# Loading q and k of heads 0 to 3 in two token ranges, and storing the last rows in three pieces, in a sliding-window attention and gated MLP kernel

## Chip, cores and metric

The kernel runs on one core of a Trainium2 chip. The metric is the time of one execution on the device in microseconds (us), here the median of three. Lower is better.

## The reference

Causal attention over a window of 64 tokens (8 batches, 8 heads, 576 tokens, head size 64), and behind it a gated MLP on the 4608 tokens of width 512 with 1536 hidden units. Inputs and output are fp32.

```python
scores = scale * np.matmul(q, k.transpose(0, 1, 3, 2))
rel = pos[:, None] - pos[None, :]
mask = (rel >= 0) & (rel < 64)
scores = np.where(mask, scores, -1e9)
attn = softmax(scores)                       # max taken off, sum + 1e-9
x = np.matmul(attn, v).transpose(0, 2, 1, 3).reshape(B * S, H * D)
gate = np.maximum(x @ w_gate, 0.0)
return gate * (x @ w_val) @ w_out            # [4608, 512]
```

## The kernel before

**Units and tiles.** Attention is computed in units of 192 tokens (`U`), three to a batch, later in quads of 256. The MLP works on tiles of tokens: four of 384 (two units each), then six of 512. A unit goes through `u_st` (scores, transposed, as 64-token blocks against 128 keys), `u_exp` (ScalarE), a mask or, for units 0 and 1, a bias that `u_bias` puts into PSUM ahead of the scores, `u_pv` (probabilities times values, with a column of ones that yields the sum), `u_recip` and `u_norm` (VectorE) and `u_turn`, a VectorE transpose that writes the tile `xt` that the MLP reads. `hidden` multiplies `xt` with the gate and value weights into PSUM tiles of one bank each (pool `f_ps`, four banks in rotation), ScalarE applies the relu (L453), VectorE multiplies the two (L456) into `g_sb`, and `out_mm` multiplies that with the output weights. The 12 chunks of 128 hidden units are counted by f.

**Loads.** q, k, v and the weights come in through GpSimd's DMA queue (L148, L150, L167, L191), which casts fp32 to fp16 on the way. The exceptions are q and k of batch 0, heads 0 to 3 (`G` = 4 heads on 128 partitions, 32 partitions per head): `first_load` (L169) fetches each as one fp32 transfer of 128 rows of 4608 bytes on SyncE's queue (L172), and `first_round` (L174) casts it to fp16, half of the columns on VectorE and half on ScalarE. `qk_trans` (L180) then transposes blocks of 32 x 32 pairs on VectorE into `kT` and `qT`, which the scores read. A partition holds 18 consecutive tokens of a head. Heads 4 to 7 (`hh` = 1) are loaded by GpSimd (`qk_load`) right after and take only the transpose.

**Order of the work.** Every engine works through its instructions in the order in which the program writes them. The head of the kernel (L537 to L590) is written out by hand: loads, constants, bias, casts and transposes of k and q, scores and exps of units 0 and 1, `v_spread` (copies values to the other half of the partitions, VectorE for unit 0, GpSimd for unit 1), `u_pv` and normalisation of both units. Units 0 and 1 are tokens 0 to 383 of batch 0; unit 2, its last 192 tokens, is planned later. After that a planner, `Weaver`, takes over: `W.at(t, fn)` puts a piece of work at time t of a clock that counts TensorE's matmuls and the estimated landing of weights (`w_need`), and `hidden` and `out_mm` write out whatever has come due before each group of their own matmuls. So the plan's times fix only the order in each engine's stream. Relus and gates are put into the plan at the clock of their matmuls. From `W.advance(15.3)` (L660) on, the first tile's hidden chunks f = 0 to 3 come in two spans of 192 tokens (gate weights for both spans, then value weights for both), then chunks 4 to 11 with 384 tokens at a time. Unit 2's scores are planned at 26.0 (L591).

**The last rows.** `output_last` (L505) computes the last 128 rows in two column halves of 256 (L514), so that the copy and store of the first half run beside the matmuls of the second. The second half is copied in two parts, ScalarE and VectorE, and stored on two queues (L520, L521). The copies use `o_sb`, a pool of three buffers that the earlier output copies (L488) use too.

Of the kernel before, what the change touches and what calls it, by code (L numbers as in the profile page):

```python
# [10 lines left out]
FP32 = mybir.dt.float32  # L11
FP16 = mybir.dt.float16
# [32 lines left out]
def kernel(  # L45
# [10 lines left out]
    nc = tc.nc  # L56
    B, H, S, D = q.shape
    DM = H * D
# [7 lines left out]
    G = 4  # L66
    scale = 1.0 / float(D) ** 0.5
    TT = 2 * U
# [4 lines left out]
    starts = [TT * t for t in range(NS)] + [NS * TT + WT * t for t in range(NL)]  # L73
# [15 lines left out]
    wo = persist.tile([128, NF, DM], FP16)  # L89
# [76 lines left out]
        src = (q if name == "q" else k)[b, G * hh:G * hh + G]  # L166
        nc.gpsimd.dma_start(tile_, src.rearrange("h (i j) d -> (h i) (j d)", i=32))  # L167

    def first_load(name):  # L169

        t32 = nat["32", name] = x_sb.tile([128, S // 32 * D], FP32, name=f"{name}32", bufs=1)
        nc.sync.dma_start(t32, (q if name == "q" else k)[0, 0:G].rearrange("h (i j) d -> (h i) (j d)", i=32))  # L172

    def first_round(name, copies):  # L174
        n = S // 32 * D // len(copies)
        to = nat[0, name, 0] = a_in.tile([128, S // 32 * D], FP16, name=f"{name}0", bufs=2)
        for i, copy in enumerate(copies):
            copy(to[:, n * i:n * i + n], nat["32", name][:, n * i:n * i + n])  # L178

    def qk_trans(b, name, hh, j0=0, j1=S // 32):  # L180

        src = nat[b, name, hh].bitcast(FP32).rearrange("p (j e) -> p j e", e=32)
        dst = qTs[b % 2][:, hh] if name == "q" else kTs[b % 2][:, hh, 64:64 + S]
        dst = dst.bitcast(FP32).rearrange("p c o -> p (c o)")
        nc.vector.transpose(dst.rearrange("p (i j) -> p j i", i=32)[:, j0:j1], src[:, j0:j1])  # L185
# [8 lines left out]
    def v_spread(u, copy=None, h0=0, h1=H):  # L194

        b, uu = divmod(u, UB)
        t = v16s[b % 2]
        copy = copy or nc.vector.tensor_copy
        for g0, g1 in (((0, 3),), ((4, 5),), ((6, 7),))[uu]:
            copy(t[64:128, g0:g1:2, h0:h1, 0:64], t[0:64, g0 + 1:g1 + 1:2, h0:h1, 0:64])  # L200
        for g0, g1 in (((2, 3),), ((4, 5),), ((6, 9),))[uu]:
            copy(t[0:64, g0:g1:2, h0:h1, 0:64], t[64:128, g0 - 1:g1 - 1:2, h0:h1, 0:64])  # L202
# [73 lines left out]
    def u_pv(u, hhs=(0, 1), banks=None):  # L276

        d = units[u]
        if "pv" not in d:
            if banks:  # L280
                d["pv"] = [one_bank("pv") for _ in range(2)]
            else:
                both = two_banks("pv")
                d["pv"] = [both[:, hh] for hh in range(2)]
                d["both"] = both
        for hh in hhs:
            to = d["pv"][hh]
            for w in range(UB):
                b, vw = divmod(UB * u + w, NG)
                for s in range(2):  # L290
                    for j in range(G):
                        c = VW * (2 * w + s)
                        nc.tensor.matmul(  # L293
                            to[32 * j:32 * j + 32, c:c + D + 1], p_of(u, G * hh + j, w)[:, 32 * s:32 * s + 32],
                            v16s[b % 2][:, vw, G * hh + j, 0:D + 1],
                            start=True, stop=True, skip_group_check=True)
        return 0.27 * len(hhs)
# [195 lines left out]
    def op_tile():  # L493
        return f_ps.tile([128, DM], FP32, name="op", tag="h")
# [10 lines left out]
    def output_last(t):  # L505

        last = widths[t] // 128 - 1
        output(t, range(last))
        W.drain()
        for col in range(2):  # L510
            op = op_tile()
            for f in range(NF):
                g_sb, _ = gs[t]
                nc.tensor.matmul(op[:, 0:256], g_sb[:, f, bass.ds(last * 128, 128)], wo[:, f, 256 * col:256 * col + 256],  # L514
                                 start=(f == 0), stop=(f == NF - 1))
            parts = ((0, 256, nc.scalar.copy, nc.sync),) if col == 0 else (
                (0, 128, nc.scalar.copy, nc.scalar), (128, 256, nc.vector.tensor_copy, nc.sync))
            for c0, c1, copy, queue in parts:
                o_sb = f_sb.tile([128, DM], FP32, name="o_sb")
                copy(o_sb[:, c0:c1], op[:, c0:c1])  # L520
                queue.dma_start(out[bass.ds(starts[t] + last * 128, 128), 256 * col + c0:256 * col + c1], o_sb[:, c0:c1])  # L521

    def output_by_rows(t):
        ops = [op_tile() for _ in range(TT // 128)]
# [8 lines left out]
    with tc.manual_schedule():  # L533
# [170 lines left out]
```

The softmax here doesn't subtract the row's maximum and nothing guards it: scores larger than these inputs give would overflow.

## Time and profile before

The median is 324.95 us (324.91 to 325.01). The profiled execution spans 323.3 us.

| Engine | busy us | share of the span |
|---|---|---|
| TensorE, matmuls | 313.7 | 97% |
| VectorE | 192.1 | 59% |
| ScalarE | 127.0 | 39% |
| GpSimd | 93.7 | 29% |

| Group (line, engine) | number | mean ns | busy us |
|---|---|---|---|
| hidden matmuls (L468, TensorE) | 1088 | 338 and 335 | 223.8 |
| output matmuls (L482, TensorE) | 420 | 379 | 93.9 |
| gate (L456, VectorE) | 120 | 631 | 75.4 |
| transposes of q and k, 128x576 (L185, VectorE) | 32 | 1245 and 1237 | 39.2 |
| output stores (SyncE's queue) | 35 | 2.8 us to landing | |

In the table a row of the profile's groups is one line of the program on one engine; mean ns is the duration of one instruction. Matmuls overlap, so their durations are longer than the distance from one to the next. In lines of the profile "out<-in" names the tile written and the tile read; "idle before, <-releaser" is how long the engine had nothing to do and what ended that. In the timeline a line begins with start and duration in us. A DMA issue has its duration on the issuing engine, and separately the time from issue to landing. For DMA queues, q1 is the queue of SyncE and q0 that of GpSimd; the three figures are packets, megabytes written and the share of the stretch that 16 engines spent on them.

### The profile page before, as it was taken

The page shows a single profiled execution, that of the slowest core. Times are in us where ns is not written, and L with a number is a line of the kernel's source. Part 1 is how long each engine was busy: PE and PEld are TensorE (multiplying, and loading weights), DVE is VectorE, ACT ScalarE, POOL GpSimd, SP SyncE. Part 2 cuts the span into 40 slices and gives each one's busy share as a digit, 9 for nine tenths or more (in the row PEclk, how much of TensorE's full clock was granted, in tenths as well). Part 3 has the DMA queues.
Part 4 walks back from the last instruction along what each step waited for, and adds up shares of the span by engine and source line. Part 5 has one row for each costly group of instructions (what it writes and reads, how often), then busy time and mean ns, then how long its engine had stood idle before and what let it go on. Part 6 is the DMA issues. An engine that isn't in the chain of part 4 may idle for free.

```text
span 323.3 us, 8901 instructions
## 1 busy us (share of the span) xinstructions
PE 313.7 (97%) x3851; PEld 168.4 (52%) x3851; DVE 192.1 (59%) x370; ACT 127.0 (39%) x249; POOL 93.7 (29%) x138
## 2 busy tenths in 40 slices
PE   5699999999999999999999999999999999999995
PEld 2586958656556644454445444454445444544443
DVE  5947962687938749564755656674767146723410
ACT  3444324534424523532454234613372237223321
POOL 8766335285900390029000910071000000000000
PEclk9599999999999999999999999999999999999999
DMA  7999998989590269019900892091001200020002
GB/s 215 186 196 210 194 107 174 155 150 163 83 211 4 15 108 181 3 12 124 214 5 2 111 203 24 2 122 70 0 2 38 97 0 2 21 111 3 0 34 98
DMA packets 52488, 29.48 MB, mean 91 GB/s; under 512 B 38880, under 2 KB 43872, under 8 KB 52448
## 3 DMA queue, kind: packets, MB, share of 16 engines
q0 software_dynamic: 46688, 18.29, 48.4%
q1 hardware_dynamic: 5616, 10.55, 8.9%
q8 instruction: 30, 0.49, 0.6%
q10 hardware_dynamic: 144, 0.07, 0.1%
q14 instruction: 10, 0.08, 0.1%
HBM read 37.75 MB, written 9.44 MB: 146 GB/s over the span
## 4 chain that ended last, share of the span: by engine, by line
PE 94%; DMA 2%; POOL 2%; issue 0%; ACT 0%; DVE 0%; DVEq 0%; POOLq 0%
PE h L468 59%; PE op L482 28%; PE st L233 3%; PE pv L371 2%; DMA v<-in_v_dram 2%; PE pv L293 1%; POOL v L191 1%; DMA out_dram<-o_sb 1%; POOL k L167 0%; POOL v L200 0%; POOL v L202 0%; ACT o_sb L489 0%; POOL q L167 0%; PE st L207 0%; POOL ident L107 0%
## 5 line engine op out<-in xcount | busy, mean ns | idle before, releaser
L456 DVE TENSOR_TENSOR g_sb<-r_sb,h 128x512 f16<-128x512 f32 (+1 forms) x120 | 75.4, 631 | 86.3 <-PE h L468 84.5
L468 PE MATMUL h<-xt,wg 128*128 128x512 f16 (+2 forms) x544 | 112.5, 338 | 0.1
L468 PE MATMUL h<-xt,wv 128*128 128x512 f16 (+2 forms) x544 | 111.3, 335 | 0.0
L453 ACT ACTIVATE r_sb<-h 128x512 f32<-128x512 f32 (+1 forms) x120 | 66.7, 558 | 89.5 <-PE h L468 80.4
L482 PE MATMUL op<-wo,g_sb 128*128 128x512 f16 x420 | 93.9, 379 | 0.0
L468 PEld LDWEIGHTS <-wg 128*128 128x128 f16 x544 | 51.5, 99 | 42.8 <-issue 0.5
L468 PEld LDWEIGHTS <-wv 128*128 128x128 f16 x544 | 50.5, 98 | 40.8
L482 PEld LDWEIGHTS <-g_sb 128*128 128x128 f16 x420 | 40.3, 98 | 47.1
L191 POOL DMA_DIRECT2D v<-in_v_dram x41 | 34.5, 861 | 95.0 <-PE pv L371 90.1
L489 ACT COPY o_sb<-op 128x512 f32<-128x512 f32 x35 | 20.5, 586 | 84.7 <-PE op L482 84.5
L356 DVE TENSOR_TENSOR pw<-pw,mask 128x512 f16<-128x512 f16 x48 | 19.3, 422 | 14.6 <-ACT pw L352 14.3
L352 ACT ACTIVATE pw<-st 128x512 f16<-128x512 f32 x48 | 25.7, 605 | 5.0 <-PE st L233 4.5
L200 POOL COPY v<-v 64x512 f16<-64x512 f16 (+1 forms) x21 | 15.5, 736 | 24.3 <-DMA v<-in_v_dram 23.4
L185 DVE STREAM_TRANSPOSE kT<-k 128x576 f32<-128x576 f32 x16 | 19.9, 1245 | 0.2 <-ACT k L178 0.2
L185 DVE STREAM_TRANSPOSE qT<-q 128x576 f32<-128x576 f32 x16 | 19.3, 1237 | 0.1
L267 ACT ACTIVATE p<-st 128x384 f16<-128x384 f32 (+1 forms) x40 | 14.0, 441 | 8.2 <-PE st L233 8.2
L391 DVE TENSOR_TENSOR xw<-pv,rw 128x448 f16<-128x448 f32 (+1 forms) x36 | 16.2, 507 | 0.4
L233 PE MATMUL st<-qT,kT 32*128 32x64 f16 x1152 | 12.9, 192 | 3.5 <-DVE qT L185 3.5
L202 POOL COPY v<-v 64x512 f16<-64x512 f16 (+1 forms) x21 | 15.9, 759 | 1.0
L233 PEld LDWEIGHTS <-kT 32*128 32x128 f16 x1152 | 10.8, 94 | 10.5 <-issue 8.5
L396 DVE STREAM_TRANSPOSE xt<-xw 128x1024 f16<-128x1024 f16 x12 | 14.9, 1244 | 0.4
L272 DVE TENSOR_TENSOR p<-p,mask 128x384 f16<-128x384 f16 x24 | 9.5, 414 | 3.6 <-ACT p L267 3.5
(46 smaller groups left out, 97.9 us busy)
## 6 DMA issues: line engine op xcount, KB each, us to landing
out_dram<-o_sb SPq DMA_DIRECT2D x35, 256.0 KB, 2.8
k<-in_k_dram POOLq DMA_DIRECT2D x15, 288.0 KB, 5.7
q<-in_q_dram POOLq DMA_DIRECT2D x15, 288.0 KB, 8.6
v<-in_v_dram POOLq DMA_DIRECT2D x31, 128.0 KB, 8.9
wg<-in_moe_w_gate_dram POOLq DMA_DIRECT2D x6, 256.0 KB, 6.4
wv<-in_moe_w_val_dram POOLq DMA_DIRECT2D x6, 256.0 KB, 7.7
wo<-in_moe_w_out_dram POOLq DMA_DIRECT2D x3, 512.0 KB, 12.2
v<-in_v_dram POOLq DMA_DIRECT2D x10, 64.0 KB, 5.8
```

The costliest lines, as they stand in the source:

```text
L185: nc.vector.transpose(dst.rearrange("p (i j) -> p j i", i=32)[:, j0:j1], src[:, j0:j1])
L191: nc.gpsimd.dma_start(v16s[b % 2][lo:hi, g, :, 0:64], v[b, :, 64 * g - 64 + lo:64 * g - 64 + hi].rearrange("h p d -> p h d"))
L202: copy(t[0:64, g0:g1:2, h0:h1, 0:64], t[64:128, g0 - 1:g1 - 1:2, h0:h1, 0:64])
L233: return [lambda dh=dh: nc.tensor.matmul(to, kTs[b % 2][rows, hh, 64 * w:64 * w + 128, dh], qTs[b % 2][rows, hh, 64 * w:64 * w + 64, dh], ...
L352: nc.scalar.activation(d["p"][g].rearrange("p n c -> p (n c)"), d["st"][g], ACT.Exp, scale=scale)
L356: nc.vector.tensor_tensor(p, p, mask[:, None, :].to_broadcast([128, 2 * QW, 64]), MUL)
L391: nc.vector.tensor_tensor(d["x"][:, hh, s0:s1], pv[:, :, 0:D].rearrange("p s (c e) -> p s e c", e=2), d["r"][:, hh, s0:s1, :, None].to_bro ...
L453: nc.scalar.activation(part(r_sb), part(h1), ACT.Relu)
L456: nc.vector.tensor_tensor(g_sb[:, f:f + w, c0:c0 + n], part(r_sb), part(h2), MUL)
L468: nc.tensor.matmul(h[:, b * n:b * n + n], wt[:, c, (f + b) * 128:(f + b) * 128 + 128], xt[:, c, c0:c0 + n], start=(c == 0), stop=(c == NC ...
L482: nc.tensor.matmul(op, g_sb[:, f, bass.ds(sub * 128, 128)], wo[:, f], start=(f == 0), stop=(f == NF - 1))
L489: nc.scalar.copy(o_sb, op)
```

## The change

q and k of heads 0 to 3 are no longer one transfer each. The first 384 tokens, those of units 0 and 1, are loaded ahead, and the other 192 tokens, which only unit 2 uses, later: two small memsets on VectorE, written behind unit 0's `u_pv`, touch the tiles of the later part, so that its loads on SyncE wait until VectorE has come that far. Since a token range of several heads can't be put on 128 partitions by one access pattern, each part is loaded head by head, four transfers of 32 partitions (3072 bytes per row for the first part, 1536 for the second). Casts and transposes follow the parts: those of the first part stand where they stood, a third shorter, and those of the second are put into the plan at 19.0 to 19.9, the cast on ScalarE alone. A partition now holds 12 consecutive tokens of the first range and 6 of the second. The purpose is to have fewer bytes and shorter VectorE work ahead of the first scores.

In `output_last` the last 128 rows come in three column pieces of 256, 128 and 128, so that what is copied and stored after the last matmul is half as wide, and each copy has a buffer of its own (`consts`) in place of the rotating `o_sb`.

```diff
-    def first_load(name):
-        t32 = nat["32", name] = x_sb.tile([128, S // 32 * D], FP32, name=f"{name}32", bufs=1)
-        nc.sync.dma_start(t32, (q if name == "q" else k)[0, 0:G].rearrange("h (i j) d -> (h i) (j d)", i=32))
+    def part_tile(name, t0, t1):
+        parts[name, t0] = consts.tile([128, (t1 - t0) // 32 * D], FP32, name=f"{name}32_{t0}")
+
+    def part_load(name, t0, t1):
+        src = q if name == "q" else k
+        for g in range(G):
+            nc.sync.dma_start(parts[name, t0][32 * g:32 * g + 32], src[0, g, t0:t1].rearrange("(i j) d -> i (j d)", i=32))
+
+    def part_round(name, t0, t1, copies):
...
+            copy(to[:, c0 + n * i:c0 + n * i + n], parts[name, t0][:, n * i:n * i + n])
+
+    def part_trans(name, t0, t1):
...
+        nc.vector.transpose(dst.rearrange("p (i j) -> p j i", i=32), src)
...
-        for col in range(2):
+        for c0, c1 in ((0, 256), (256, 384), (384, DM)):
...
+            halves = ((0, n // 2, nc.scalar.copy, nc.scalar), (n // 2, n, nc.vector.tensor_copy, nc.sync))
+            for i, (a0, a1, copy, queue) in enumerate(halves if c1 == DM else ((0, n, nc.scalar.copy, nc.sync),)):
+                o_sb = consts.tile([128, a1 - a0], FP32, name=f"o_last{c0}_{i}")
...
         for name in "kq":
-            first_load(name)
+            for t0, t1 in ((0, TT), (TT, S)):
+                part_tile(name, t0, t1)
+            part_load(name, 0, TT)
...
-        first_round("k", (dve, act))
+        part_round("k", 0, TT, (dve, act))
         u_bias(0)
         u_bias(1)
-        qk_trans(0, "k", 0)
-        first_round("q", (act, dve))
-        qk_trans(0, "q", 0)
+        part_trans("k", 0, TT)
+        part_round("q", 0, TT, (act, dve))
+        part_trans("q", 0, TT)
...
             u_pv(0, (hh,), True)
+        for name in "kq":
+            nc.vector.memset(parts[name, TT][:, 0:1], 0.0)
+            part_load(name, TT, S)
...
+        for i, name in enumerate("kq"):
+            W.at(19.0 + 0.6 * i, lambda name=name: part_round(name, TT, S, (act,)))
+            W.at(19.3 + 0.6 * i, lambda name=name: part_trans(name, TT, S))
         W.at(26.0, lambda: u_st(2))
```

More of the change, by code (lines that the diff above doesn't have):

```diff
@@ L167, in qk_load @@
         nc.gpsimd.dma_start(tile_, src.rearrange("h (i j) d -> (h i) (j d)", i=32))
[L169 to L178 removed]
+    parts = {}
+    def part_tile(name, t0, t1):
[5 more added lines that the diff above has]
+    def part_round(name, t0, t1, copies):
+        if (0, name, 0) not in nat:
+            nat[0, name, 0] = a_in.tile([128, S // 32 * D], FP16, name=f"{name}0", bufs=2)
+        to, c0, n = nat[0, name, 0], t0 // 32 * D, (t1 - t0) // 32 * D // len(copies)
+        for i, copy in enumerate(copies):
+            copy(to[:, c0 + n * i:c0 + n * i + n], parts[name, t0][:, n * i:n * i + n])
+    def part_trans(name, t0, t1):
+        src = nat[0, name, 0][:, t0 // 32 * D:t1 // 32 * D].bitcast(FP32).rearrange("p (j e) -> p j e", e=32)
+        dst = qTs[0][:, 0] if name == "q" else kTs[0][:, 0, 64:64 + S]
+        dst = dst.bitcast(FP32).rearrange("p c o -> p (c o)")[:, t0:t1]
+        nc.vector.transpose(dst.rearrange("p (i j) -> p j i", i=32), src)
     def qk_trans(b, name, hh, j0=0, j1=S // 32):
@@ L509, in output_last @@
         W.drain()
-        for col in range(2):
+        for c0, c1 in ((0, 256), (256, 384), (384, DM)):
             op = op_tile()
+            n = c1 - c0
             for f in range(NF):
                 g_sb, _ = gs[t]
-                nc.tensor.matmul(op[:, 0:256], g_sb[:, f, bass.ds(last * 128, 128)], wo[:, f, 256 * col:256 * col + 256],
+                nc.tensor.matmul(op[:, 0:n], g_sb[:, f, bass.ds(last * 128, 128)], wo[:, f, c0:c1],
                                  start=(f == 0), stop=(f == NF - 1))
[L516 to L521, printed above, removed]
+            halves = ((0, n // 2, nc.scalar.copy, nc.scalar), (n // 2, n, nc.vector.tensor_copy, nc.sync))
+            for i, (a0, a1, copy, queue) in enumerate(halves if c1 == DM else ((0, n, nc.scalar.copy, nc.sync),)):
+                o_sb = consts.tile([128, a1 - a0], FP32, name=f"o_last{c0}_{i}")
+                copy(o_sb, op[:, a0:a1])
+                queue.dma_start(out[bass.ds(starts[t] + last * 128, 128), c0 + a0:c0 + a1], o_sb)
     def output_by_rows(t):
```

## The prediction

> **What bounds the kernel now.** I read the page's busy rows first: TensorE is busy 97% of the span, so only the start, the end and holes between can give time. Next the chain of waits, cut to the first 62 us:
>
> ```profile
> 6.29 5.55 DMA v<-in_v_dram
> 11.99 0.64 POOL v L200
> 12.69 0.62 POOL v L202
> 13.35 0.74 PE pv L293 x39
> 14.67 2.25 PE h L468 x15
> 17.03 9.48 PE h L468 x81
> ```
>
> The last of unit 1's values lands at 11.84, GpSimd spreads them, pv and one heating matmul follow, the first hidden matmul starts at 14.67. From 17.03 TensorE never stops; what shifts there shifts the end. The timeline of the first 20 us shows the other strand, q:
>
> ```profile
> 0.81 0.38 SPq L172 DMA_DIRECT2D k<-in_k_dram  x1
> 1.25 0.42 SPq L172 DMA_DIRECT2D q<-in_q_dram  x1
> 1.31 0.69 POOL L167 DMA_DIRECT2D k<-in_k_dram  x1 [0.79 <-POOLq L688]
> 6.26 0.67 ACT L178 CAST q<-q 128x576 f16<-128x576 f32 x1 [0.70 <-DMA q<-in_q_dram]
> 7.60 1.26 DVE L185 STREAM_TRANSPOSE qT<-q 128x576 f32<-128x576 f32 x1
> 9.78 1.23 DVE L185 STREAM_TRANSPOSE qT<-q 128x576 f32<-128x576 f32 x1
> 16.27 1.03 DVE L327 STREAM_TRANSPOSE xt<-x 128x384 f16<-128x384 f16 x2
> ```
>
> VectorE works almost without a pause from q's landing to unit 1's turn, which ends at 17.30 and which TensorE waits for at 16.93. So two strands end within half a microsecond: v's landing, and q's landing plus VectorE.
>
> Third, the queues, in the stretch 3:4, then 4:5:
>
> ```profile
> q1 hardware_dynamic: 89, 0.35, 101.2%
> q0 software_dynamic: 8, 0.02, 9.6%
> ```
>
> The engines are full. SyncE's k and q (1.18 MB) go first; GpSimd's k of heads 4 to 7, issued at 1.31, moves no packet before 4.75. On an idle queue such a load shows packets 1.2 us after issue (issued 48.21, packets from 49.4), so it was ready at about 2.5 and stood behind SyncE's backlog. The reverse is seen at 48 to 53 us: an output issued on SyncE at 48.82, just behind a k load, moves nothing while that load runs (stretch 51.2:51.6, then 52.4:52.8), and lands after 4.9 us instead of 2:
>
> ```profile
> q0 software_dynamic: 33, 0.08, 107.5%
> q1 hardware_dynamic: 72, 0.14, 92.9%
> DMA to landing us min/median/max: 4.9/4.9/4.9
> ```
>
> Transfers are served about in order of arrival, whole load by whole load, whichever queue they are on.
>
> **What the Trainium skill says.** "DMA: Bandwidth & Descriptors", Queues, rings and completion order: an engine takes its queues in turn and leaves one only at a packet boundary (9 to 17 descriptors typically). A GpSimd load of 128 rows is 8 rows per engine, about one such turn; the trace at 48 to 53 us agrees. Same page, Issuing engines are not separate DMA queues: all share 16 engines; agrees. "TensorE: Matmul & The Clock Gate", Part 1: the clock falls to half after an idle window of some 3.4 us and comes back after a busy one; here the granted clock is 0.50 from 9.6 to 16.4, two such windows. An earlier start may lift it a window sooner, but that gives TensorE speed only where weights bind it (case B), so I count nothing for it.
>
> **The head, part by part.** Two issues on SyncE become eight (32 rows x 3 KB). Issue cost: no row has 32 rows. The issue rows show 0.33 us for outputs of 64 to 256 KB alike and 0.38 to 0.42 for the first two, start to start 0.44 (0.81 to 1.25). Bounds: 0.1 (a quarter, if it goes by rows) to 0.44 (fixed). I take 0.44, as the output's cost doesn't go by size. Then the last q piece is issued at 0.81 + 7 x 0.44 = 3.9. With 0.95 us to the first packet (issued 0.81, packets from about 1.75) pieces arrive at 1.8, 2.2, 2.6, 3.1 (k) and 3.5, 4.0, 4.4, 4.8 (q). GpSimd's k (2.5) and q (2.00 + 1.2 = 3.2) get ahead of the last k piece and of all of q. Ahead of or in the last q piece are then 0.79 + 2 x 0.59 = 1.97 MB read, at about 0.36 MB per us: 1.8 + 5.5 = 7.3, plus 0.5 (q moved its bulk by 5.5 and landed at 6.26): 7.8 against 6.26.
>
> VectorE gains: casts and transposes of k and q fall to 2/3. The q cast is 0.80 x 2/3 = 0.53, the transposes start 1.09 apart, 0.73 for the short one. From q's landing L: transpose at L + 0.63, the two of heads 4 to 7 at L + 1.36 and L + 2.45, done at L + 3.68. With L = 7.8 that is 11.48, against 11.01: 0.47 late, and everything up to unit 1's turn with it. k's short work is hidden ahead of q. Break-even is L = 7.3. Each DMA adds 16 completion packets (a load of 128 rows shows 144 packets), 192 more in the two stages; small, and left inside the 0.5.
>
> v's landing moves the other way: of its bytes ahead, 0.39 MB (1.1 us) are gone; with gaps between SyncE's pieces 0.9 us, so 10.95.
>
> **The tail of q and k.** Two memsets (0.06 us each, like that of `warm`) go behind the value copies, which end at 12.16: 12.6 + 0.1 = 12.75. SyncE's eight pieces (49 KB) wait for them; nothing else is queued on SyncE until the first output at 48.8, so the wait itself holds up nobody. They are issued from 12.8 to 15.9, the last arriving at 16.7. By then GpSimd has issued, 0.9 us earlier than in the trace, four halves of the second weight chunk; the last (15.34 before) at 14.45, arriving 15.65. So the last q piece stands behind much of them. They landed at 20.95 (14.64 + 6.3) and 23.2 (15.34 + 7.9) with the same bytes ahead; I take between, 22.1.
>
> Who waits: by the plan's clock, ScalarE's rounding of q (19.6) stands ahead of the relus of fc 4 to 7, and VectorE's transposes (19.3, 19.9) between the second and third gate of fc 0 to 3. The third gate frees the PSUM bank of the third tile of fc 4 to 7, started at 21.14 + 2 x 0.65 = 22.44. From the landing L2: cast 0.45 (the exp of 128x384 at L267 takes 0.44), transpose 0.43 (a third of 1.24), gate 0.56, four handoffs of 0.05: that tile starts at L2 + 1.64. TensorE is late by L2 - 20.8: 0.15 at 20.95, 1.3 at 22.1, 2.4 at 23.2. This replaces the 0.47, as it is a place in time, not a sum. If L2 is below 20.3 the two casts and transposes fit the idle 19.2 to 22.0 of ScalarE and the gates' slack, and cost nothing.
>
> **The last rows.** 12 matmuls of 256 become 24 of 128. Those of 256 take 2.78/24 = 0.115; at 192 columns 1.32/16 = 0.083. For 128, bounds 0.056 and 0.081 ("TensorE: Matmul & The Clock Gate", Back-to-back issue gap; the trace has none); at 0.064, 24 x 0.064 - 12 x 0.111 = +0.2 us (0 to +0.6). Copies: ScalarE 0.27 to about 0.21, VectorE 0.29 to 0.23. VectorE's last copy started at 320.34 though matmuls ended at 319.88: its `o_sb` buffer waited for an output that landed at 319.92. A buffer of its own removes 0.37. Last issue: 319.88 + 0.2 + 0.09 + 0.23 + 0.03 = 320.43 against 320.66: 0.2 gained (-0.2 to +0.4).
>
> **The rivals.** *A, the likeliest: the pieces fall behind GpSimd's loads.* 324.95 + 1.3 - 0.2 = 326.05, from 325.3 to 327.2. For it: arrival order at both places of the trace. Against: the issue cost is unseen for 32 rows.
>
> *B, the pieces keep ahead (cheap issue, or queues shared finely).* q lands before 6.3, both strands come about 1 us earlier. But weights then bind: the second half of fc 8 to 11's gate weights lands at 18.28 + 8.3 = 26.6, whatever order 1.18 MB of q and k took before it, and its first user, the third matmul of the tile at 26.92, ran at 27.24. So at most 0.64 - 0.1 = 0.55 is kept. 324.95 - 0.55 - 0.2 = 324.2. For it: VectorE work that surely goes. Against: arrival order.
>
> *C, a wash:* the head loses or gains little, the tail lands near 21, and the end gives its 0.2: 324.8, from 324.3 to 325.3.
>
> **Numbers.** A 0.58, B 0.29, C 0.13. Predicted is A, 326.1. The range runs from B's 324.2 less some of its end (324.1) to A's upper bound 327.2. Faster by over 0.2% (below 324.3) is B, 0.29; same is C, 0.13; slower is A, 0.58.
>
> **What would show it.** Right: eight issues 0.4 apart; ScalarE's q cast starting after 7; SyncE's last piece issued after 15 and landing after 21; ScalarE and VectorE idle behind q's load near 20 to 22; TensorE with a hole after 21.8. Wrong: q's cast before 6.3, a first hidden matmul near 13.7, and a hole only ahead of a weight chunk; or a last issue no earlier after the last matmul.

## The result: slower, and the profile after

The changed kernel takes 328.36 us (median; 327.97 to 329.86), the kernel before 324.95: ratio 1.0115, with an interval of 1.0093 to 1.0138. That is 3.4 us more, where 1.15 more was predicted. The direction was right and the size lies outside the range. The profiled execution is the changed kernel's slowest, with a span of 328.2 us; a second profile of the same kernel, from another chip, spans 326.5 and is used below beside it. One execution of a later kernel, of 473.6 us at a granted clock of 0.66, is left out of all figures, and its profile with it.

The page first. The chain by line, and the costliest PE group, the gate matmuls, with its idle time last:

```profile
PE h L481 56%; PE op L495 27%; DMA q<-in_q_dram 3%; PE st L246 3%; PE pv L384 2%; SPq L178 1%; DVE p L285 1%; PE pv L306 1%; PE op L528 1%; DVE x L330 1%; DVE qT L191 0%; DVE v L213 0%; DVE v L215 0%; DVE qT L198 0%; ACT q L185 0%
...
L481 PE MATMUL h<-xt,wg 128*128 128x512 f16 (+2 forms) x544 | 113.4, 340 | 1.5 <-DVE g_sb L469 1.3
```

The hidden matmuls cost almost what they did (340 and 335 ns against 338 and 335; the 2 ns are 0.9 us of busy time, and the clock, further below, accounts for most of it), so most of the time went where TensorE stood still. The load of q has taken a place on the chain, and there is one new hole of 1.3 us. Both are in the first 30 us. Lines from the timeline of that stretch (start, duration, engine, line), with SyncE's issues, then what waits for them:

```profile
0.81 1.78 SPq L178 DMA_DIRECT2D k<-in_k_dram  x4
1.31 0.70 POOL L167 DMA_DIRECT2D k<-in_k_dram  x1 [0.79 <-POOLq L709]
2.64 2.01 SPq L178 DMA_DIRECT2D q<-in_q_dram  x4
8.04 0.51 ACT L185 CAST k<-k 128x384 f16<-128x384 f32 x1 [5.73 <-DMA k<-in_k_dram]
9.80 0.51 ACT L185 CAST q<-q 128x384 f16<-128x384 f32 x1 [1.25 <-DMA q<-in_q_dram]
12.11 1.24 DVE L198 STREAM_TRANSPOSE qT<-q 128x576 f32<-128x576 f32 x1
```

Eight issues stand where two were, about 0.46 us from start to start. k's cast begins at 8.04 (before 4.89), q's at 9.80 (before 6.26), although a third fewer bytes were asked for. VectorE's last transpose ends at 13.35 instead of 11.01, and the first hidden matmul starts at 17.14 instead of 14.67. The 32 gate matmuls of fc 0 to 3, before and after:

```profile
14.67 3.99 PE L468 MATMUL h<-xt,wg 128*128 128x192 f16 x32
17.14 4.71 PE L481 MATMUL h<-xt,wg 128*128 128x192 f16 x32 [0.20 <-DVE xt L340]
```

They take 0.72 longer. TensorE's granted clock is 0.50 until 16.4 in the trace before, and until 21.1 in this one. In the second profile it is 0.50 until 17.6, and fc 0 to 3 takes no longer than before.

Why q is late although it is smaller can be read from the queues. The stretch 3:4 (packets, MB written, share of 16 engines), which was full of SyncE's packets before:

```profile
q0 software_dynamic: 36, 0.08, 48.8%
q1 hardware_dynamic: 14, 0.04, 13.9%
```

Together 63% instead of 101%: four of SyncE's pieces have been issued and wait, yet the engines are a third idle. From issue to landing the four k pieces take 2.1, 2.1, 3.8 and 5.8 us, the four q pieces 5.5 to 5.7. The first two k pieces arrive ahead of GpSimd's loads; every later one waits about as long as those loads last. Why these pieces wait while the engines have room is not shown.

Then the deferred part. The chain of waits through it:

```profile
19.71 5.77 DMA q<-in_q_dram
25.58 0.52 ACT q L185
26.12 0.52 DVE qT L191
26.64 0.40 DVE g_sb L469
27.08 4.06 PE h L481 x24
```

The last q piece is issued at 19.71 and lands at 25.5; its cast and transpose stand ahead of a gate on VectorE, and the third tile of fc 4 to 7 waits for that gate: 27.08 instead of 22.44. Behind the head and the clock it would have started at about 25.6, so the hole costs 1.45.

A third, smaller place was in none of the cases. Unit 3's masks on VectorE and GpSimd's first copy of the values of units 4 and 5, before, then after:

```profile
42.01 1.51 DVE L272 TENSOR_TENSOR p<-p,mask 128x384 f16<-128x384 f16 x4 [0.41 <-ACT p L267]
45.24 0.61 POOL L200 COPY v<-v 64x512 f16<-64x512 f16 x1 [9.56 <-DMA v<-in_v_dram]
46.66 3.09 DVE L285 TENSOR_TENSOR p<-p,mask 128x384 f16<-128x384 f16 x4 [0.41 <-ACT p L280]
46.45 0.61 POOL L213 COPY v<-v 64x512 f16<-64x512 f16 x1 [9.40 <-DMA v<-in_v_dram]
```

Before, the four masks took 1.51 us and were over at 43.5, ahead of GpSimd's copies, which began at 45.24. The late head pushed them together: 3.09 us, and the matmuls behind pv(3) came 0.63 later still.

The sum closes. Unit 2's scores start at 31.08 (before 26.44), 4.64 late: 2.47 from the head, 0.72 from the clock, 1.45 from the hole. With the masks' 0.63 the matmuls of the last rows start 5.28 late (322.38 against 317.10); from there to the end it takes 5.8 us instead of 6.15. The span grows by 4.9. In the second profile the head costs 2.2 (first hidden matmul 16.89), the hole 1.4 (1.25 of it idle), and neither the clock nor the masks cost anything: unit 2's scores start at 30.06, the last rows 3.67 late, and the span is 3.3 more, close to the median's 3.4.

### The profile page after: what moved, and what is told of

Read it like the earlier page. It is cut to its first block, busy times and chain, and to the rows that moved or that the text cites. A ratio compares the mean times of both kernels' runs of the same rounds, so it can differ in the third digit from the quotient of the medians.

```text
span 328.2 us, 8958 instructions
## 1 busy us (share of the span) xinstructions
PE 315.9 (96%) x3863; PEld 169.8 (52%) x3863; DVE 194.8 (59%) x374; ACT 127.7 (39%) x252; POOL 93.8 (29%) x138
## 4 chain that ended last, share of the span: by engine, by line
PE 89%; DVE 4%; DMA 3%; SPq 1%; issue 1%; ACT 1%; ACTq 0%
PE h L481 56%; PE op L495 27%; DMA q<-in_q_dram 3%; PE st L246 3%; PE pv L384 2%; SPq L178 1%; DVE p L285 1%; PE pv L306 1%; PE op L528 1%; DVE x L330 1%; DVE qT L191 0%; DVE v L213 0%; DVE v L215 0%; DVE qT L198 0%; ACT q L185 0%
## 5 line engine op out<-in xcount | busy, mean ns | idle before, releaser
L481 PEld LDWEIGHTS <-wg 128*128 128x128 f16 x544 | 52.3, 100 | 44.4 <-issue 2.2
L198 DVE STREAM_TRANSPOSE kT<-k 128x576 f32<-128x576 f32 x15 | 18.7, 1245 | 0.0
L198 DVE STREAM_TRANSPOSE qT<-q 128x576 f32<-128x576 f32 x15 | 18.1, 1237 | 0.0
L285 DVE TENSOR_TENSOR p<-p,mask 128x384 f16<-128x384 f16 x24 | 12.0, 539 | 2.9 <-ACT p L280 2.8
```

What stands on the lines that cost most here:

```text
L481: nc.tensor.matmul(h[:, b * n:b * n + n], wt[:, c, (f + b) * 128:(f + b) * 128 + 128], xt[:, c, c0:c0 + n], start=(c == 0), stop=(c == NC ...
```

## The experiments

The theory after the result: the split into eight issues costs the head, because pieces that arrive behind GpSimd's loads wait for them, and what is late there comes back at the deferred part. The rivals: the shape of the pieces (32 rows), the deferral itself, the place of its casts in the plan, and the end. TensorE's clock has no kernel of its own; where it takes part, the text gives what the traces show. Each ratio is to the kernel before on the same chip.

| Kernel | q's cast | first hidden | unit 2's scores | ratio (interval) |
|---|---|---|---|---|
| before | 6.26 | 14.67 | 26.44 | 1 |
| after (second chip) | 9.53 | 16.89 | 30.06 | 1.0122 (1.0105 to 1.0139) |
| eight pieces, nothing deferred | 10.65 | 18.42 | 30.88 | 1.0159 (1.0144 to 1.0175) |
| GpSimd's loads 1 us later | 10.22 | 17.42 | 30.60 | 1.0128 (1.0113 to 1.0143) |
| q's first pieces on ScalarE's queue | 8.93 | 16.86 | 29.78 | 1.0125 (1.0108 to 1.0142) |
| deferred casts planned later | 9.41 | 16.68 | 29.35 | 1.0075 (1.0061 to 1.0088) |
| GpSimd's loads held back 2.6 us | 6.80 | 15.26 | 28.17 | 1.0044 (1.0028 to 1.0060) |
| held back, and planned later | 6.35 | 15.12 | 27.91 | 1.0052 (1.0038 to 1.0066) |

### The split alone, and its shape

The first kernel is the one before with k and q in four transfers each, whole rows, nothing deferred.

```diff
-        nc.sync.dma_start(t32, (q if name == "q" else k)[0, 0:G].rearrange("h (i j) d -> (h i) (j d)", i=32))
+        for g in range(G):
+            nc.sync.dma_start(t32[32 * g:32 * g + 32], (q if name == "q" else k)[0, g].rearrange("(i j) d -> i (j d)", i=32))
```

> The kernel before with k and q of heads 0 to 3 loaded head by head, eight transfers of 32 rows of 4608 bytes, nothing deferred and nothing else changed. Arrival order (pieces issued 0.46 us apart fall behind GpSimd's two loads of heads 4 to 7): q's cast starts at about 9.8 to 10.8 instead of 6.26, the first hidden matmul near 18, no hole in TensorE near 25; 327.5 to 328.5. If the deferred tail alone costs the time: 325.0.

330.29 us, ratio 1.0159. Its timeline:

```profile
10.65 0.67 ACT L179 CAST q<-q 128x576 f16<-128x576 f32 x1 [2.02 <-DMA q<-in_q_dram]
18.42 4.68 PE L469 MATMUL h<-xt,wg 128*128 128x192 f16 x32
```

The bytes and the destination are those of the kernel before, and q's cast is 4.4 us later. Again the first two pieces land 2.6 and 2.8 after their issue and the others after 4.1 to 6.3. So the split alone makes the kernel slower than the whole change does, which fits that the change's third fewer bytes give some of it back. The time is 2 us above what was expected. In the profile the last rows are 5.0 late: 3.75 are the head, 0.7 the clock (0.50 until 22.3), and 0.55 unit 3's masks, which met GpSimd's copies here too (2.46 us for four).

The second kernel has the same bytes in eight transfers again, each of all 128 rows and a quarter of the columns (1152 bytes).

```diff
+        n = S // 32 * D // 4
+        for g in range(G):
+            nc.sync.dma_start(t32[:, n * g:n * g + n], (q if name == "q" else k)[0, 0:G].rearrange("h (i j) d -> (h i) (j d)", i=32)[:, n * g:n * g + n])
```

> As the run with eight transfers of 32 rows, and the same bytes and number of transfers, but each transfer is a quarter of the columns on all 128 rows (1152 bytes per row). Arrival order by the number of issues: as late as with 32 rows, q's cast at 9.8 to 10.8, 327.5 to 328.5. If it is the narrow shape[...] that makes the pieces slow: q's cast near 7 to 7.5 and 325 to 326.

330.06 to 331.27 us, ratio 1.0166 (1.0149 to 1.0182), again some 2 us above what was expected; q's cast can't be given. The ratio is that of the pieces of 32 rows. So full height does not help, and the narrow shape is not what makes the kernel slow; the number of issues, and so the arrival of the later ones, is what the two kernels share. That a row of 1152 bytes has a cost of its own is not excluded here; the two kernels that follow show narrow pieces that are quick.

### Who gets ahead of whom

Here, in the changed kernel, GpSimd issues its loads of heads 4 to 7 behind its mask work instead of ahead of it.

```diff
-        for name in "kq":
-            qk_load(0, name, 1)
         warm = consts.tile([128, 2], FP32)
...
         bands()
+        for name in "kq":
+            qk_load(0, name, 1)
```

> The changed kernel with GpSimd's two loads of k and q of heads 4 to 7 issued after the mask work (about 4.0 and 4.7) instead of at 1.3 and 2.0, so that SyncE's eight pieces meet no other load. If standing behind these loads makes the pieces late: each piece lands about 2.1 to 2.6 us after its issue, as the first k piece did, q's cast starts at 6.4 to 6.9 instead of 9.8, the first hidden matmul near 15, the deferred q lands near 20 and the hole near 26 is gone; 324.6 to 325.5. If the number of issues or the narrow shape makes them slow by itself: q's cast stays at 8 or later, 327 or more.

329.32 us, a miss: no gain, and q's cast at 10.22, because the edit moved the loads by 1 us only: they now arrive behind k's pieces and still ahead of q's. Its timeline tells more than its time:

```profile
2.27 0.69 POOL L167 DMA_DIRECT2D k<-in_k_dram  x1
4.36 0.51 ACT L185 CAST k<-k 128x384 f16<-128x384 f32 x1 [2.06 <-DMA k<-in_k_dram]
10.22 0.51 ACT L185 CAST q<-q 128x384 f16<-128x384 f32 x1 [5.35 <-DMA q<-in_q_dram]
```

All four k pieces now land 2.1 us after issue and k's cast comes at 4.36 instead of 8.04. q's pieces, issued from 2.63, land after 4.0 to 6.1 us. One queue, one size of piece, and exactly those that arrive ahead of GpSimd's load are quick.

The next kernel holds GpSimd's loads back further, behind a memset of a scratch tile (1.7 us of extra work that nothing reads); they are gone from their old place, as above.

```diff
         bands()
+        hold = consts.tile([128, 1900], FP16)
+        nc.gpsimd.memset(hold, 0.0)
+        for name in "kq":
+            qk_load(0, name, 1)
```

> The changed kernel with GpSimd's loads of k and q of heads 4 to 7 behind the mask work and a GpSimd memset of a scratch tile that fills the time to about 3.8, so that they reach the engines after all eight pieces (in the run that moved them by one microsecond only, k's pieces alone went ahead and landed 2.1 us after issue, q's stood behind and landed after 4.0 to 6.1). Arrival order: q's four pieces land 2.1 to 2.5 us after issue too, q's cast starts at 6.2 to 6.6 instead of 9.3 to 10.2; the values now set the first hidden matmul, near 14.7 to 15.2; the deferred q still lands near 20 to 21.5, so a hole of 0 to 0.7 us may stay: 324.8 to 326.0. If q is late for another reason than GpSimd's loads: q's cast at 9 or later, 328 or more.

326.19 us, ratio 1.0044, just above what was expected: about two thirds of the loss is gone. Its timeline, then its queue in 3:4:

```profile
3.89 0.69 POOL L167 DMA_DIRECT2D k<-in_k_dram  x1
6.80 0.51 ACT L185 CAST q<-q 128x384 f16<-128x384 f32 x1 [1.84 <-DMA q<-in_q_dram]
23.19 2.45 PE L481 MATMUL h<-xt,wg 128*128 128x384 f16 x14 [0.71 <-DMA wg<-in_moe_w_gate_dram]
```

```profile
q1 hardware_dynamic: 97, 0.20, 66.1%
```

All eight pieces land 2.0 to 2.7 us after issue. This settles the head: it is the arrival behind GpSimd's loads. It also shows the floor of the split. With nothing in their way eight pieces move 0.20 MB in that stretch, where two whole loads moved 0.35; a piece of 96 KB (0.098 MB) every 0.46 us comes to 0.21 MB per us. Whether the shape of 32 rows holds them back as well can't be told from this. So q is no earlier than before (6.80 against 6.26) with a third fewer bytes. And holding back has its own price: GpSimd's other issues come 1.1 us later, its values land at 12.7 instead of 11.84, and fc 4 to 7 waits 0.71 for a weight chunk, which takes 8.4 us to land instead of 5.7; it was issued at 14.77, among the deferred pieces.

The last of this group gives q's first pieces to ScalarE's queue, so that all eight are issued by 2.6.

```diff
-            nc.sync.dma_start(parts[name, t0][32 * g:32 * g + 32], src[0, g, t0:t1].rearrange("(i j) d -> i (j d)", i=32))
+            (nc.scalar if name == "q" and t0 == 0 else nc.sync).dma_start(parts[name, t0][32 * g:32 * g + 32], src[0, g, t0:t1].rearrange("(i j) d -> i (j d)", i=32))
```

> The changed kernel with the four first q pieces issued on ScalarE's queue, beside k's four on SyncE, so that all eight are issued by 2.6 instead of 4.65. Arrival order: pieces issued at 1.7 and 2.2 stand behind one or both of GpSimd's loads as k's third and fourth did (landing near 5.5 and 8.0), so q is complete near 8.0, about 1.7 us earlier than in the changed kernel and still later than the 6.26 before; 325.5 to 326.5. If the count of issues doesn't matter: unchanged, 328.2.

328.85 us, ratio 1.0125, a miss. q's last piece landed at 8.59, where about 8.0 was expected, but k's cast came only at 8.52 (6.66 in the changed kernel on that chip): pieces of k and q alternate, so the last k piece stands behind q's. Of the pieces the first pair lands after 2.6 to 3.0 us, the last pair after 6.2 to 6.4. The Trainium skill ("DMA: Bandwidth & Descriptors", Issuing engines are not separate DMA queues) says that a second issuer saves only issue time; the run agrees, and here that time was worth nothing.

### The deferred part

The changed kernel with the deferred casts and transposes 5.6 us later in the plan:

```diff
-            W.at(19.0 + 0.6 * i, lambda name=name: part_round(name, TT, S, (act,)))
-            W.at(19.3 + 0.6 * i, lambda name=name: part_trans(name, TT, S))
+            W.at(24.6 + 0.6 * i, lambda name=name: part_round(name, TT, S, (act,)))
+            W.at(24.9 + 0.6 * i, lambda name=name: part_trans(name, TT, S))
```

> The changed kernel with the casts and transposes of the deferred 192 tokens planned at 24.6 to 25.5 instead of 19.0 to 19.9, so that they stand behind the gates of chunks 0 to 3. If the wait for the deferred q in front of these gates makes the hole in TensorE near 26: the hole of 1.3 us goes, chunk 4 to 7 runs through from 24.3, about 326.7. If the hole is only where the late head shows and weights would stop TensorE anyway: unchanged, 328.2.

327.53 us, ratio 1.0075, on a third chip; the changed kernel's ratios on the two others are 1.0115 and 1.0122. The gates no longer stand behind q, and fc 4 to 7 runs through, as expected. The time is still 0.8 above the 326.7 expected: a smaller wait has come ahead of unit 2's scores.

```profile
23.35 2.76 PE L481 MATMUL h<-xt,wg 128*128 128x384 f16 x16
29.35 0.55 PE L246 MATMUL st<-qT,kT 32*128 32x64 f16 x48 [0.64 <-DVE qT L191]
44.92 1.51 DVE L285 TENSOR_TENSOR p<-p,mask 128x384 f16<-128x384 f16 x4 [0.40 <-ACT p L280]
```

The masks have their 1.51 us back without having been touched: they end at 46.43, GpSimd's copies begin at 46.70. The times of this kernel spread over 0.1 us, those of the changed kernel on the second chip over 1.4. That would fit a hole whose length hangs on the landing of one piece; it was not followed, and the clock may have a part in it.

Both edits together:

> As the run with GpSimd's loads held back to 3.8, and the deferred casts and transposes planned at 24.6 to 25.5. Arrival order and the hole as the two causes: both are gone, no hole near 26, TensorE in step with the kernel before (first hidden matmul near 14.7 to 15.2, scores of unit 2 near 26.5), 324.6 to 325.5. If a third cause holds the changed kernel back: above 326.

326.91 us, ratio 1.0052, a miss: no better than holding back alone. In its profile the hole and the weight wait are gone, but values land at 12.58 as in the other, and unit 2's scores wait 0.65 for q, as they did with the late plan alone. This profile is of an execution 0.9 us shorter than the others; whether those had the weight wait is open.

The changed kernel with the value copies of units 4 and 5 on VectorE instead of GpSimd:

```diff
-            W.at(52.0, lambda u=u: v_spread(u, pool))
+            W.at(52.0, lambda u=u: v_spread(u, dve))
```

> The changed kernel with the value copies of units 4 and 5 on VectorE instead of GpSimd. If GpSimd's copies slow unit 3's masks (772 ns each beside them, 359 ns alone), the masks take 0.36 us each again, pv of unit 3 waits for nothing, and 0.6 us come back against the changed kernel on the same chip, when its masks fall on the copies there too. If the masks are slow for another reason: they stay near 770 ns and the time stays.

329.78 us, ratio 1.0145 (1.0130 to 1.0160). The masks take 1.51 us. On this chip that is little, as they took 1.80 in the changed kernel: there three of the four masks took 0.36 each, and the fourth, nearly all of it beside a copy, 0.65. In the first profile copies ran beside all four, and they took 0.61 to 1.19 each. With the masks of the late plan, quick and clear of the copies, this puts their slowness down to GpSimd's copies. The time does not fall: VectorE now does the copies itself, and at 59.07 TensorE waits 0.48 for a gate behind them. The Trainium skill ("SBUF — State Buffer", Who interferes with whom) says that a VectorE instruction with two inputs in SBUF contends with a GpSimd instruction that reads SBUF. A mask reads two tiles (p and mask) and a copy reads v; 3.09 against 1.51 us agrees.

For these comparisons the changed kernel was run again on the same chip:

> The changed kernel as it is, on the chip of this comparison: near 328, with q's cast at 9.3 to 9.8 and the hole near 26. It is what the other three are compared with.

329.16 us, ratio 1.0122.

### The halving without the split

If eight issues are the cost, two transfers of the same bytes should bring what the change was for. The section on the change says that no one access pattern puts a token range of several heads on 128 partitions. That is not so: a pattern of three steps (head, row, bytes) does it in one transfer:

```diff
-        for g in range(G):
-            nc.sync.dma_start(parts[name, t0][32 * g:32 * g + 32], src[0, g, t0:t1].rearrange("(i j) d -> i (j d)", i=32))
+        nc.sync.dma_start(parts[name, t0], src[0, 0:G, t0:t1].rearrange("h (i j) d -> h i (j d)", i=32))
```

> The changed kernel with each part of k and q in one transfer of all four heads (128 rows, source pattern of three steps: head, row, bytes): two issues ahead and two deferred ones instead of eight and eight; all else as after. Theory (the eight issues, whose later pieces arrive behind GpSimd's loads, cost the head, and the halving of bytes is sound): k and q arrive at about 1.8 and 2.2, ahead of GpSimd's at 2.5; 0.79 MB at 0.35 MB per us after 1.8, plus 0.5, is 4.6 for q; q's cast starts at 4.6 to 5.3 (before 6.26), the first hidden matmul at 13.7 to 14.6 (before 14.67). The deferred q, planned at 19.6, lands near 21 among the weights and leaves a hole of 0 to 1.2 us. Time 324.3 to 325.5. Rival (one transfer with such a pattern is as slow as its four pieces, or a deferred part costs as much wherever the head stands): q's cast at 6.5 or later, or a hole of over 1.2 us; 326.0 to 328.5.

340.39 us, ratio 1.0482 (1.0455 to 1.0508), far outside both expectations. The timeline, and SyncE's queue in the stretch 4:5:

```profile
10.72 0.51 ACT L184 CAST k<-k 128x384 f16<-128x384 f32 x1 [8.42 <-DMA k<-in_k_dram]
17.75 0.51 ACT L184 CAST q<-q 128x384 f16<-128x384 f32 x1 [6.51 <-DMA q<-in_q_dram]
```

```profile
q1 hardware_dynamic: 30, 0.09, 27.0%
```

SyncE's share is about a quarter. Counting the packets of these two transfers by start and duration, at most four are under way in 97.5% of the time that any is (7.1 of 14.5 us at exactly four); in the kernel before it is most often sixteen. And each of the two shows four completion packets, where each load of the kernel before shows sixteen. The Trainium skill states the rule ("DMA: Bandwidth & Descriptors", Why a DMA increments its semaphore by 16 and not by 1): a transfer is spread over the largest number of engines, up to 16, that divides the outermost size of both its patterns. Here these are 4 heads and 128 partitions: four engines. The trace agrees. With the deferred casts at 23.0 to 23.9:

> As the kernel with one transfer per part, and the deferred casts and transposes planned at 23.0 to 23.9 instead of 19.0 to 19.9, between those of after and those planned at 24.6. Theory: with q landing early and the deferred q landing before 23, neither end of the deferral is on TensorE's path: no wait for q ahead of the gates of fc 0 to 3, none ahead of unit 2's scores; unit 2's scores at 26.0 to 26.4 (before 26.44); 324.0 to 324.7. Rival (what is deferred has to be paid later, by weights and values landing behind it, whatever the plan): a new wait of over 0.5 us for weights or for unit 2's q, 325.0 to 326.5.

335.86 us, ratio 1.0328 (1.0314 to 1.0342), again far outside both; q's cast at 15.81, that of the deferred q at 33.54. So the two-issue form is no way out.

Is it the pattern or the queue? Two kernels load k and q of heads 0 to 3 on GpSimd's queue, ahead of heads 4 to 7 and straight to fp16: the first whole, with the ordinary pattern, the second in two parts, with the pattern of three steps.

```diff
-            first_load(name)
+            qk_load(0, name, 0)
...
-        first_round("k", (dve, act))
-        first_round("q", (act, dve))
```

> The kernel before, with k and q of heads 0 to 3 loaded whole (576 tokens, one transfer each) by GpSimd's queue, ahead of heads 4 to 7, straight to fp16; SyncE's loads and the casts on ScalarE and VectorE fall away. GpSimd's other issues come 1.25 us later. It is the base for the kernel of the next run. GpSimd's first load shows packets 1.2 us after issue, so k at 2.5, q at 3.2: 1.18 MB at 0.35 MB per us, q at 6.2 to 6.8; its transpose at that time (before 7.0 after a cast), values 0.8 us later as in the run with GpSimd's loads held back: 12.6. First hidden matmul 15.0 to 15.5; 325.0 to 325.8.

326.02 us, ratio 1.0036 (1.0024 to 1.0049), 0.2 above what was expected; q's transpose at 7.03, values copied from 12.77, first hidden matmul 15.17. Of the second kernel's edit the load is shown:

```diff
+        nc.gpsimd.dma_start(nat[0, name, 0][:, t0 // 32 * D:t1 // 32 * D],
+                            src[0, 0:G, t0:t1].rearrange("h (i j) d -> h i (j d)", i=32))
```

> The same, with the first 384 tokens ahead and the other 192 behind unit 0's values, one transfer each with the pattern of three steps, straight to fp16, so that the halving of bytes stands without eight issues. If the slowness of one transfer with that pattern belongs to the pattern (four heads, four engines): q's transpose after 10, first hidden matmul after 17, 328 us or more. If it belongs to SyncE's queue alone: q's transpose at 5.2 to 6.0, values about 1 us earlier than in the kernel with whole loads, first hidden matmul 14.0 to 14.6 and 0.5 to 1.2 us less than that kernel: 324.2 to 325.2. If halving is worth nothing: within 0.3 of that kernel.

329.83 us, ratio 1.0145 (1.0131 to 1.0158). Its timeline, against 5.59 and 7.03 for whole loads:

```profile
9.01 0.85 DVE L193 STREAM_TRANSPOSE kT<-k 128x384 f32<-128x384 f32 x1 [3.28 <-DMA k<-in_k_dram]
10.44 0.85 DVE L193 STREAM_TRANSPOSE qT<-q 128x384 f32<-128x384 f32 x1 [0.59 <-DMA q<-in_q_dram]
```

With two thirds of the bytes k is 3.4 us later. The pattern is slow on this queue too. What the halving would bring with transfers that are neither split nor narrow stays open: no kernel here had both.

### The end

The kernel before with only the last rows in three pieces, as in the changed kernel's `output_last`:

> The kernel before with only the last rows changed (pieces of 256, 128 and 128 columns, buffers of their own). Theory of the trace after: from the end of the last full output group to the end of the span it saves about 0.35 us (323.30 - 317.28 = 6.02 before, 328.2 - 322.54 = 5.66 after), so about 324.6. Rival: twelve more matmuls eat it, 324.9 to 325.2.

325.70 us against 325.05, ratio 1.0028 (1.0017 to 1.0039): slower, where 0.35 less was expected. SyncE's last issue does come earlier, at 320.52 (before 320.66), and lands at 322.0. But the program closes with SyncE's waits on one semaphore after another, some 0.06 us each when nothing is outstanding. What those waits (L699) stood for, first in this kernel:

```profile
SPq L699 <- DMA out_dram<-o_last: 1.1, 1, 1.1
```

and in the kernel before:

```profile
SPq L699 <- DMA out_dram<-o_sb: 0.8, 2, 0.4
```

Before, seven of the nine waits pass at 321.0 to 321.5 while the stores are still under way, and the two that need them come last. With three pieces the outstanding store is the second in the order, and the other seven wait behind it until 322.9, 0.9 us after the landing; 0.45 of that is a single pause between two of them, for which the profile names no cause. From the first matmul of the last rows to the end it is 6.65 us here, 6.15 before, and 5.8 in the changed kernel, where the order is the good one again. The same edit thus cost 0.65 us in one program and shortened the end by 0.4 in another. The traces put that down to the order; no kernel changed the order alone.

The kernel before with its two column halves, and only a buffer of its own for each last copy:

```diff
-                o_sb = f_sb.tile([128, DM], FP32, name="o_sb")
+                o_sb = consts.tile([128, DM], FP32, name=f"o_last{col}_{c0}")
```

> The kernel before with its two last column halves as they are, and only the buffers of the last copies their own instead of the rotating three. VectorE's last copy then starts about 0.37 us earlier (319.97 for 320.34). If the end of the span follows the last store: about 324.65. If the end is set by the order in which the closing waits are gone through, as where three pieces alone were 0.65 us slower although the last store was issued earlier: anywhere from 324.65 to 325.7, with the gap between the last landing and the end of the span in the trace as the sign.

324.88 against 324.99, ratio 1.0000 (0.9991 to 1.0008): no change beyond the interval. The last copies:

```profile
319.93 0.27 ACT L520 COPY o_last<-op 128x128 f32<-128x128 f32 x1 [0.94 <-PE op L514]
...
320.23 0.29 DVE L520 COPY o_last<-op 128x128 f32<-128x128 f32 x1 [9.93 <-ACT o_last L520]
```

VectorE still starts when ScalarE's copy of the same tile ends, 0.35 after the matmuls. It starts 0.11 earlier than before (320.34), not 0.37: it was hardly waiting for the buffer. What ties it to ScalarE's copy was not tried.

## Why the prediction was right in direction and wrong in size

**Arrival order: right.** Eight issues at 0.46 (predicted 0.44), GpSimd's loads ahead of the last k pieces and all of q: the traces of the changed kernel and of the three with GpSimd's loads moved show it piece by piece. By the prediction's own times GpSimd's k (2.5) is ahead of the third k piece (2.6) too, and that piece took 3.8 us. Case B's sign, q's cast before 6.3, is in no trace of a kernel with eight pieces.

**The failed step: "Ahead of or in the last q piece are then ... 1.97 MB read, at about 0.36 MB per us".** q landed at 9.7, not 7.8. Which bytes go ahead was right, but they were not moved at that rate from the start. 0.36 is the rate of engines filled by two whole loads. With SyncE's pieces trickling in and GpSimd's load just starting, 3:4 ran at 63%, and SyncE's pieces waited meanwhile. The run with GpSimd held back shows that eight pieces alone reach only 0.20 to 0.22 MB per us. Counting the packets splits the 1.9 us. The two queues together had read 1.97 MB by about 8.1 instead of 7.3: 0.8. From there to the landing 1.6 passed, where the prediction adds 0.5: the last of q's packets ended only at 8.76, as GpSimd's value loads, whose small packets began at 7.8, had come in among them, and q counted as landed 0.94 after that. This last step took 0.29 in the kernel before, 0.34 with GpSimd held back, and 0.93 again in the kernel with eight pieces and nothing deferred. Why it is longer beside the value loads was not tried.

From there on the prediction's chain held: VectorE is done 3.65 behind q's landing (predicted 3.68), so its +0.47 became 2.3. "k's short work is hidden ahead of q" held too, though barely: k's last piece waited 5.8 us, k was cast at 8.04, and its transpose ended at 9.42. One sum is off without consequence: fourteen transfers more are 224 completion packets, not 192.

**The tail: formula right, landing wrong.** "That tile starts at L2 + 1.64": measured L2 + 1.58 (25.5, 27.08). "TensorE is late by L2 - 20.8" gives 4.7 for 25.5, and 4.64 was measured; in the second profile L2 is 24.46, which gives 3.7, and 3.6 was measured. But L2 was taken as 22.1 and bounded at 23.2 by weight landings of the kernel before, with a head 0.47 late. With VectorE 2.3 late the memsets came late too: the first piece was issued at 15.21 instead of 12.8 (2.4 of the 3.4 us by which L2 missed). The issues then came 0.64 apart, not 0.44 (four k issues took 2.9 us), so that the last was issued at 19.71 instead of 15.9 (1.4 more), and the landing took 0.4 less than assumed. Why these issues were slower was not tried. The prediction let the tail "replace" the head's lateness as a place in time. That held; the later start merely moved the place, so that the hole came on top of the head. This is why the range failed: its upper end took the tail's worst case behind a head that was 0.47 late.

**v's landing: wrong.** Predicted 0.9 earlier, it came 0.5 later (12.37 against 11.84; 11.91 in the second profile). The 0.39 MB taken from ahead of it were worth nothing while the engines stood a third idle; that this is the whole reason wasn't tried by itself.

**The end: the right gain by luck.** SyncE's last issue followed the end of the last full output group by 3.18 us instead of 3.38: 0.20, as predicted. But two terms of that sum were wrong and cancelled. The matmuls were to cost 0.2 more; they start 0.056 apart at 128 columns, the lower of the prediction's two bounds, and 0.109 at 256, and the last rows' matmuls together take 2.81 instead of 2.78. The buffer of its own was to give 0.37; it gave 0.1, as the run shows. The profile had said so, with ScalarE's copy named as the releaser, and the prediction overrode it. And the order of the closing waits, to which the traces put down that the same edit lengthened the end by 0.5 in one program and, with the earlier issue, shortened it by 0.4 in another, was in no step of the prediction.

**Not foreseen:** the masks beside GpSimd's copies, up to 0.63 us, a consequence of the late head. And the clock: the prediction counts nothing for a start that is earlier, and says nothing of one that is later. In the first profile it came back at 21.1, 3.9 behind the first hidden matmul, and 0.7 us went; in the second at 17.6, 0.7 behind it, and nothing did.

Of the second profile's 3.7 us ahead of the last rows, then, 2.2 are the head and 1.4 the hole; the end gives about 0.4 back. The late plan takes the hole away and holding GpSimd back most of the head, each shown by its own run. Together they don't add up: the late plan puts a wait of 0.65 ahead of unit 2's scores in place of the hole, and the loads that were held back bring the values later. None of the kernels tried is faster than the kernel before by more than its interval.

## What to carry to other kernels

Count issues, not only bytes: a transfer cut in four is four arrivals, and here each that came behind another queue's load waited for it, though it was only 96 KB; the third of the bytes that was saved brought nothing here. Before costing a transfer at the full rate, ask whether enough is queued to fill the engines in that stretch, and on how many engines its outermost dimension puts it (the rule above). Don't stop at the last byte: here the landing came up to 0.9 us behind the last packet. If an estimate makes a strand late, carry that lateness into everything that is issued behind it before bounding the next step.

## What the runs showed of the hardware that was not expected

- Pieces of 96 KB, issued 0.46 us apart on SyncE with nothing in their way, moved 0.20 to 0.22 MB per us, against 0.35 for whole loads of 576 KB; behind a GpSimd load the same piece took 3.8 to 6.1 us to land instead of 2.0 to 2.7.
- From SyncE's last packet of q to its landing it took 0.3 us with whole loads and with GpSimd held back, and 0.9 where GpSimd's value loads ran beside it.
- A transfer of 128 partitions whose source pattern begins with 4 heads kept at most four packets under way in 97.5% of its time, where the ordinary one kept mostly sixteen: q's cast at 17.75 instead of 6.26.
- Pieces of 32 partitions and pieces of 128 partitions with a quarter of the columns made the kernel equally slow (1.0159 and 1.0166).
- SyncE went through its closing waits in a fixed order; where an outstanding store came second, the waits behind it took 0.9 us more after its landing.
- TensorE's granted clock came back from 0.50 at 16.4, 17.6 and 21.1 us in the kernel before and in two profiles of the changed one; in the last, 32 gate matmuls took 4.71 us instead of 3.99.
- A mask on VectorE took 0.36 us alone and 0.61 to 1.19 where a GpSimd copy ran beside most of it.
- VectorE's copy of one half of a PSUM tile began when ScalarE's copy of the other half ended, with separate buffers as well (320.23 after 319.93 + 0.27).
